# Layer 2's second block of rows: a step's seven w_ch1 products in one run, its w_ch2 products in one run

## The chip, the cores and the metric

One core of one Trainium2 chip runs the whole program once. The metric is device time in microseconds (us), from the program's start to its end. Times below come from three timed runs of the kernel before and from one profiled execution of it; in the trace, times count from the start of the span.

## The reference, cut to what matters

Three layers follow each other: a retention attention, a gated unit (`moe`), and a plain two-matrix layer (`moe2`). The change concerns the last one:

```python
def _moe2_ref(x, g_ln, w_ch1, w_ch2):          # x: (4, 576, 512)
    mu = np.mean(x, axis=-1, keepdims=True)
    var = np.mean((x - mu) ** 2, axis=-1, keepdims=True)
    xn = (x - mu) / np.sqrt(var + 1e-06) * g_ln
    ch = np.maximum(xn @ w_ch1, 0.0) @ w_ch2   # w_ch1: 512 x 2048, w_ch2: 2048 x 512
    return (x + ch)
```

## The kernel before

The 2304 rows are 18 tiles of 128, worked on as three blocks of six tiles (blocks 0, 1, 2; 768 rows each). Every fp32 product is made of three fast ones: each operand is kept as a rounded high piece (ScalarE's cast) and a low piece (the operand minus the high piece), and `mm3` multiplies high by high, high by low and low by high, one matmul each.

For `xn @ w_ch1` a scheme of seven products in place of eight is used: rows and columns are halved, sums and differences of the weight pieces (`mix_w1`) and of the features (`mix_features`) are formed first, and `HIDDEN` names the seven products. One product is 6 matmuls with 384 columns into one of two free PSUM banks. VectorE and ScalarE add the partial results (`u`, `t`), take the relu into `h` (high piece on ScalarE, low piece on VectorE).

The work of layer 2 is a row of 24 steps `s`: 8 steps for each block, a step for each pair of 128 hidden units. Steps 0 to 7 are block 0, steps 8 to 15 block 1, steps 16 to 23 block 2. Blocks 0 and 1 multiply `h` by `w_ch2` at once (`project`): six PSUM banks `o_t` hold the sums of the block, and four calls per step (`q` = 0 to 3, 9 matmuls of 512 columns each) add to them. Block 2 keeps all its hidden values (`hidden_kept`) and multiplies at the end (`multiply_kept`), with pieces of `w_ch2` that `turn_steps` and `save_w2` have written to `wb_dram` before.

Nothing is scheduled by a tool: each engine takes its instructions in the order in which the code issues them, so the loop over `s` and `q` at the end of the kernel is the schedule. In step `s` each quarter `q` issues a part of `hidden(s)` (its two, two, two and one products), then `project(s - 1, q)`, and then the work around it:

- `split_w2`: the pieces of `w_ch2` (ScalarE cast L944, GpSimd subtraction L945) for one of the two tiles `w2_at`; `load_w2` and `save_w2` load the next and store the pieces (SyncE's DMA queue).
- `fetch_w1`: from step 8 on the pieces of `w_ch1` come back from `ws_dram`, which block 0 wrote.
- `ahead(blk, q)`: the rows of the next block, by a counter `q` that runs from 0 to 31 over a block's eight steps: load (`load_y`), normalise and transpose (`norm`), store to `z_dram`, load as features (`load_features`), scale; from 24 on `mix_features` (GpSimd, L1029) and `split_features` (ScalarE cast L1036, GpSimd subtraction L1037), one of each in a quarter.
- `turning`: the differences of the pieces of `w_ch2` for block 2, by a table of quarters: two loads, four GpSimd subtractions (L961), four casts (L964), four low pieces (L967), four stores.

Rows of 128 x 512 that are loaded or stored around the blocks share seven tiles (`row_tile`), taken in turn.

Of the kernel before, what the change touches and what calls it, by code (L numbers as in the profile page):

```python
# [31 lines left out]
TB = 6  # L32
# [69 lines left out]
def kernel(  # L102
# [878 lines left out]

    def norm(p, n):
        z = yh[n]

        def stats():
            st = numbers(p)
            yield from rstd(p, st, z, 1e-6)
            after(1, lambda: newton(st))

            def rest():  # L990
                normed(z, st)
                yield
                t = row_tile()
                dve.transpose(out=t, in_=z)
                nc.sync.dma_start(out=z_dram[n], in_=t)

            after(2, rest)

        after(0, stats)
# [173 lines left out]
    def relu(s, i, v):  # L1173
        t = h_t[s, i] = h_at[i][s % len(h_at[i])]
        act.activation(out=t[:, 0], in_=v, func=ACTF.Relu)  # L1175
        dve.scalar_tensor_tensor(  # L1176
# [3 lines left out]
    def hidden(s):  # L1180
# [5 lines left out]
        for part in ((0, 5), (1, 2), (3, 4), (6,)) if s else ((5, 0, 2, 4), (1,), (3,), (6,)):  # L1186
            for w in part:
# [9 lines left out]
                elif w == 2 or w == 4:  # L1197
                    dve.tensor_tensor(out=t, in0=v, in1=u if w == 2 else t, op=ALU.add)
                    if w == 4:
                        relu(s, 3, t)  # L1200
                else:
# [4 lines left out]
                    relu(s, {1: 0, 3: 2, 6: 1}[w], v)  # L1206
                if last:
                    free(bk[a])
            yield

# [48 lines left out]
    def project(s, q):  # L1259
# [4 lines left out]
        if p == 0 and q == 0:  # L1264
            o_t[blk] = [bank() for j in range(TB)]
        first, last = p == 0 and i == 0, p == NQ - 1 and i == 1
        w = w2_at[i]
        for j in reversed(range(TB // 2)):
# [3 lines left out]
            if last:  # L1272
                n = blk * TB + h * TB // 2 + j

                o = row_tile()
                dve.tensor_tensor(
                    out=turned_row(o), in0=ps.rearrange("p (f k c) -> p f k c", k=KE, c=32),
                    in1=o_s.pop(n).rearrange("p (f k c) -> p f k c", k=KE, c=32), op=ALU.add,
                )
                free(ps)  # L1280
                store_row(n, o)
# [112 lines left out]
    def ahead(blk, q):  # L1394
# [4 lines left out]
        if q == 1 and blk:  # L1399
            for j in reversed(range(TB // 2, TB)):  # L1400
                load_rest((blk - 1) * TB + j)
        if blk + 1 < NB:
# [25 lines left out]
        if q == 4 * NQ - 1:  # L1428
            for j in reversed(range(TB // 2)) if blk + 1 < NB else range(TB):
                load_rest(blk * TB + j)  # L1430
            if blk + 1 == NB:
                o_s[None] = row_tile()
# [30 lines left out]
    for s in range(NB * NQ):  # L1463
        if s == NK:
            keep()
        steps = hidden(s) if s < NK else hidden_kept(s)
        for q in range(4):
            next(steps)
            if 0 < s <= NK:
                project(s - 1, q)  # L1470
            if s >= NQ:
                next(turns, None)

            if q == 0 and s > 1:
                split_w2(2 * s - 1)
            if q == 1 and s > 1:
                load_w2(2 * s + 1)
                save_w2(2 * s - 1)
            if q == 2 and s:
                split_w2(2 * s)  # L1480
            if q == 3 and s:
                load_w2(2 * s + 2)
# [19 lines left out]
            ahead(*divmod(4 * s + q, 4 * NQ))  # L1502
            if q < 2 and s:
# [5 lines left out]
            else:  # L1509
                fetch_w1(s + 2, q - 1)  # L1510
    for _ in multiply_kept(NB - 1):
# [61 lines left out]
```

## Time and profile before

| what | value |
|---|---|
| median of 3 runs | 657.61 us (657.12 to 658.17) |
| the profiled execution, and its span | 658.18 us, 656.2 us |
| TensorE matmul, busy in the span | 646.8 us (99%) |
| VectorE, ScalarE, GpSimd, busy | 455.0 us (69%), 316.0 us (48%), 321.6 us (49%) |
| DMA | 181.22 MB, 276 GB/s over the span |
| granted TensorE clock | full in every slice |

The profiled execution has 2.0 us outside its span. Block 0 of layer 2 begins at 282 us, step 8 at 399 us, step 16 at 525 us, and the last product of `w_ch1` ends at 591 us. In rows of the trace, PE is TensorE, DVE VectorE, ACT ScalarE, POOL GpSimd, SPq the queue of SyncE, which issues the DMAs; `b` is any PSUM bank, `w` any of the tiles for weights, `fe` the pieces of the features.

### The profile page before, as it was taken

Reading aid. Unit: us, or ns where it says so; the run is one execution under the profiler, and the core shown is the slowest. Engines: PE = TensorE matmul, PEld = TensorE weight load, DVE = VectorE, ACT = ScalarE, POOL = GpSimd, SP = SyncE. Lnnn points to the kernel's source line nnn. Section 1 sums busy time; section 2 is a strip of 40 time slices with the busy share of each in tenths; the row PEclk is TensorE's granted clock in tenths of the full one; section 3 lists DMA queues with packets and bytes.
Section 4 is the critical chain, followed back from the end, with each engine's and each line's share of the span. In section 5 each row is a group of like instructions: output and inputs, shape, how many; then the busy total and the mean of one; then the engine's idle time right before and its main releaser. Section 6 shows DMA issues by size and latency. Waiting matters only on the chain.

```text
span 656.2 us, 12551 instructions
## 1 busy us (share of the span) xinstructions
PE 646.8 (99%) x4422; PEld 591.2 (90%) x4422; DVE 455.0 (69%) x906; ACT 316.0 (48%) x656; POOL 321.6 (49%) x315
## 2 busy tenths in 40 slices
PE   8998999999999999999999999999999999999997
PEld 5998899899889889899888999888988899999996
DVE  4698779789989885868888533555533345458894
ACT  4556795365286466434453533233535313335443
POOL 2467868225326528945655793265559743310000
PEclk9999999999999999999999999999999999999999
DMA  8999447777797695489896867799999699999634
GB/s 306 383 368 371 166 111 213 252 238 233 259 298 232 189 242 145 151 312 384 319 309 238 274 205 261 247 366 387 347 332 360 216 295 350 371 379 405 243 129 161
DMA packets 99264, 181.22 MB, mean 276 GB/s; under 512 B 9857, under 2 KB 46849, under 8 KB 97410
## 3 DMA queue, kind: packets, MB, share of 16 engines
q1 hardware_dynamic: 99202, 180.42, 81.5%
q8 instruction: 35, 0.57, 0.3%
q14 instruction: 27, 0.22, 0.1%
HBM read 122.97 MB, written 56.62 MB: 274 GB/s over the span
## 4 chain that ended last, share of the span: by engine, by line
PE 71%; DVE 3%; ACT 3%; DMA 1%; issue 1%; POOL 1%; SPq 0%; POOLq 0%; ACTq 0%; DVEq 0%
PE b L137 20%; PE b L136 20%; PE b L135 20%; PE b L864 4%; PE b L1341 3%; PE b L1342 2%; DVE c L163 1%; DMA raw<-in_w_ch_dram 1%; ACT t L695 1%; PE b L798 1%; POOL vnl L721 1%; PE b L797 0%; ACT t L692 0%; ACT raw L160 0%; DVE bs L669 0%
## 5 line engine op out<-in xcount | busy, mean ns | idle before, releaser
L137 PE MATMUL b<-fe,w 128*128 128x384 f32 x336 | 113.1, 337 | 0.0
L135 PE MATMUL b<-fe,w 128*128 128x384 f32 x336 | 112.9, 336 | 0.0
L136 PE MATMUL b<-fe,w 128*128 128x384 f32 x336 | 112.7, 335 | 0.0
L137 PE MATMUL b<-w,h 128*128 128x512 f32 (+1 forms) x270 | 98.1, 363 | 0.0
L136 PE MATMUL b<-w,h 128*128 128x512 f32 (+1 forms) x270 | 98.0, 363 | 0.0
L135 PE MATMUL b<-w,h 128*128 128x512 f32 (+1 forms) x270 | 96.8, 358 | 0.0
L945 POOL TENSOR_TENSOR w<-raw_w,w 128x512 fp32r<-128x512 f32 x30 | 39.6, 1320 | 59.0 <-ACT w L944 53.3
L135 PEld LDWEIGHTS b<-fe,w 128*128 128x128 f32 x336 | 63.1, 188 | 3.0
L136 PEld LDWEIGHTS b<-fe,w 128*128 128x128 f32 x336 | 63.1, 188 | 2.8
L137 PEld LDWEIGHTS b<-fe,w 128*128 128x128 f32 x336 | 63.0, 188 | 0.0
L137 PEld LDWEIGHTS b<-w,h 128*128 128x128 f32 x270 | 51.0, 189 | 7.6
L160 ACT ACTIVATE raw<-raw 128x512 f32<-128x512 f32 x44 | 29.9, 679 | 56.2 <-DVE b L158 49.3
L136 PEld LDWEIGHTS b<-w,h 128*128 128x128 f32 x270 | 50.9, 189 | 6.3 <-POOL w L945 0.2
L135 PEld LDWEIGHTS b<-w,h 128*128 128x128 f32 x270 | 51.0, 189 | 6.0 <-issue 0.2
L1175 ACT ACTIVATE h<-b 128x384 fp32r<-128x384 f32 x32 | 15.7, 492 | 83.8 <-DVE b L1204 54.1
L665 POOL TENSOR_TENSOR st<-st,par 128x1 f32<-128x1 f32 x36 | 22.1, 617 | 52.7 <-DVE st L664 52.2
L1176 DVE SCALAR_TENSOR_TENSOR h<-b,h 128x384 fp32r<-128x384 f32 x32 | 17.8, 556 | 30.9 <-ACT h L1175 30.9
L137 PE MATMUL b<-w_sg,vnl 128*128 128x288 f32 x128 | 37.8, 295 | 0.2 <-POOL vnl L721 0.2
L135 PE MATMUL b<-w_sg,vnh 128*128 128x288 f32 x128 | 37.8, 295 | 0.0
L137 PE MATMUL b<-xt_hi,w_in 128*128 128x288 f32 x128 | 37.7, 295 | 0.0
L136 PE MATMUL b<-w_sg,vnh 128*128 128x288 f32 x128 | 37.7, 295 | 0.0
L136 PE MATMUL b<-xt_lo,w_in 128*128 128x288 f32 x128 | 37.7, 294 | 0.0
(199 smaller groups left out, 1700.8 us busy)
## 6 DMA issues: line engine op xcount, KB each, us to landing
w<-ws_dram SPq DMA_DIRECT2D x96, 256.0 KB, 4.8
raw<-in_w_ch_dram SPq DMA_DIRECT2D x32, 512.0 KB, 5.0
ws_dram<-w SPq DMA_DIRECT2D x16, 896.0 KB, 7.4
w<-wb_dram SPq DMA_DIRECT2D x14, 1024.0 KB, 5.6
qv<-in_attn_dram SPq DMA_DIRECT2D x15, 576.0 KB, 6.8
w_dram<-c SPq DMA_DIRECT2D x32, 256.0 KB, 3.1
wb_dram<-fe SPq DMA_DIRECT2D x32, 256.0 KB, 5.1
kk<-in_attn_dram SPq DMA_DIRECT2D x15, 544.0 KB, 7.7
```

Of the source, the lines that this page charges most:

```text
L135: pe.matmul(ps, lh, rh, start=first, stop=False, skip_group_check=True)
L136: pe.matmul(ps, lh, rl, start=False, stop=False, skip_group_check=True)
L137: pe.matmul(ps, ll, rh, start=False, stop=last, skip_group_check=True)
L160: act.activation(out=f(w1), in_=f(w1), func=ACTF.Square)
L163: dve.scalar_tensor_tensor(out=f(c), in0=f(w1), scalar=F64_LEAST ** 2, in1=f(r), op0=ALU.is_ge, op1=ALU.mult)
L665: pool.tensor_tensor(out=st[:, 4:5], in0=st[:, 3:4], in1=col(par, O_MH), op=ALU.pow)
L864: pe.matmul(ps, g, wo[k][:, w], start=done[0] == 1, stop=done[0] == 3 * KE, skip_group_check=True)
L945: pool.tensor_tensor(out=t[:, 1], in0=raw, in1=f(t[:, 0]), op=ALU.subtract)
L1175: act.activation(out=t[:, 0], in_=v, func=ACTF.Relu)
L1176: dve.scalar_tensor_tensor(out=t[:, 1], in0=v, scalar=0.0, in1=f(t[:, 0]), op0=ALU.max, op1=ALU.subtract)
L1341: pe.matmul(ps, e[:, 0, x], t, start=begin, stop=False, skip_group_check=True)
L1342: pe.matmul(ps[:, 0:256], e[:, 1, x], t[:, 0:256], start=False, stop=end, skip_group_check=True)
```

## The change

For steps 8 to 15 a new function `hidden_once` issues all seven products of a step in one run (order 0, 5, 1, 2, 4, 3, 6) with a pause after the first two, in which the pieces of `w_ch2` for this same step are made: `split_w2` of both tiles. Then `project` of this step (not of the step before) follows in one run of 36 matmuls, in the order `q` = 3, 2, 0, 1; within one call the three kinds of product are now outermost and the tile `j` innermost. The four calls of `ahead`, with the turning, stand between the four calls of `project`, so all four come behind the seven products of their step. Step 7 ends with the projection of step 7 itself, in one run of 36. Step 16 has none any more.

Around it: the first result of a step passes through a tile `z` in SBUF, so that its bank comes free before its relu; `save_w2` stores from step 4 to step 11 instead of 8 to 15; the table of `turning` starts one piece every 6 quarters instead of 4 for the first five, with 4 quarters between load and use; the stores of normalised rows are collected and issued at the end of a step or ahead of the load that needs them; `load_rest` and the features' loads and scaling are called at other quarters.

```diff
     def save_w2(s):
-        if NF <= s < 2 * NK:
-            p, i = divmod(s - NF, 2)
+        if NQ <= s < NF + NQ:
+            p, i = divmod(s % NF, 2)
...
+    def hidden_once(s):
...
+        for w in (0, 5, 1, 2, 4, 3, 6):
+            x, a, first, last = HIDDEN[w]
+            if first:
+                bk[a] = bank()
+            product(s, bk[a], w, x, first, last)
+            v = bk[a][:, 0:TH]
+            if w == 0:
+                act.copy(u, v)
+            elif w == 1:
+                dve.tensor_scalar(out=z, in0=v, scalar1=0.0, scalar2=None, op0=ALU.max)
...
+            if last and w != 3:
+                free(bk[a])
+            if w == 5:
+                yield
+        relu_low(s, 2, bk[2][:, 0:TH])
+        free(bk[2])
+        relu_low(s, 0, z)
+        relu_low(s, 1, u)
+        yield
...
-    def project(s, q):
+    def project(s, q, begin=0):
...
+        for x, y in ((0, 0), (0, 1), (1, 0)) if begin and not last else ():
+            for j in js:
+                pe.matmul(
...
-            if q in (13, 20):
-                load_features(blk + 1, q // 20)
-            if q in (15 + blk, 22 + blk):
+            if q in (13, 20 - blk):
+                store_z()
+                load_features(blk + 1, q // 19)
+            if q in (15 + 2 * blk, 22 + blk):
...
-            start, pace = (3 + 4 * p, 1) if p < 5 else (8 * p - 8, 2)
-            for o in (0, 1, 1, 2, 2, 3, 4, 5):
+            start, pace = (3 + 6 * p, 1) if p < 5 else (34 + 8 * (p - 5) - p // 7, 2)
+            for o in (0, 4, 4, 5, 5, 8, 8, 9) if p < 5 else (0, 1, 1, 2, 2, 3, 4, 5):
...
-        steps = hidden(s) if s < NK else hidden_kept(s)
+        if s < NQ:
+            steps = hidden(s)
+        elif s < NK:
+            steps = hidden_once(s)
+            next(steps)
+            split_w2(2 * s + 1)
+            split_w2(2 * s)
+            load_w2(2 * s + 3)
+            load_w2(2 * s + 2)
+            next(steps)
+        else:
+            steps = hidden_kept(s)
         for q in range(4):
-            next(steps)
-            if 0 < s <= NK:
+            if NQ <= s < NK:
+                project(s, (3, 2, 0, 1)[q], 1)
+            else:
+                next(steps)
+            if 0 < s < NQ:
                 project(s - 1, q)
...
             ahead(*divmod(4 * s + q, 4 * NQ))
+            if NQ <= s < NK:
+                next(turns, None)
...
+        store_z()
+        if s == NQ - 1:
+            split_w2(2 * s + 1)
+            load_w2(2 * s + 3)
+            save_w2(2 * s + 1)
+            for q in range(4):
+                project(s, q)
```

Three places show how the instructions stand now. The first is TensorE inside a step of block 1. Rows with `fe` are products of `w_ch1`, rows with `h` products of `w_ch2`; the brackets name whom an instruction waits for. Before, the end of one call of `project` and the product behind it:

```order
L135 MATMUL b_76<-w_3373,h 128x512
L136 MATMUL b_76<-w_3373,h 128x512
L137 MATMUL b_76<-w_3373,h 128x512
L135 MATMUL b_79<-fe,w_3466 128x384 [waits DMAHW2_49,DVE_49]
L136 MATMUL b_79<-fe,w_3466 128x384
```

And now, the end of a step's second product (5) and the beginning of its third (1):

```order
L135 MATMUL b_79<-fe,w_3466 128x384
L136 MATMUL b_79<-fe,w_3466 128x384
L137 MATMUL b_79<-fe,w_3467 128x384
L135 MATMUL b_81<-fe,w_3466 128x384 [waits DMAHW6_49,Activation_49]
L136 MATMUL b_81<-fe,w_3466 128x384
```

A product follows a product now, with no projection between them, and the third waits for ScalarE's copy of the first one's result out of the same bank.

The second place is GpSimd in steps 14 and 15, where the features of block 2 are mixed and split (`mix`, `fe`), the pieces of `w_ch2` made (`w_3373`), and now some of the turning done (`raw_turn`). Before:

```order
L945 TENSOR_TENSOR w_3373<-raw_w_5348,w_3373 128x512
L1029 TENSOR_TENSOR mix<-x 128x768
L1037 TENSOR_TENSOR fe<-x,fe 128x768
L1029 TENSOR_TENSOR mix<-x,mix 128x768
L1037 TENSOR_TENSOR fe<-mix,fe 128x768
L945 TENSOR_TENSOR w_3373<-raw_w_5411,w_3373 128x512
L1029 TENSOR_TENSOR mix<-x,mix 128x768
L1037 TENSOR_TENSOR fe<-mix,fe 128x768
L1029 TENSOR_TENSOR mix<-x 128x768
L1037 TENSOR_TENSOR fe<-mix,fe 128x768
L945 TENSOR_TENSOR w_3373<-raw_w_5480,w_3373 128x512
```

And now:

```order
L945 TENSOR_TENSOR w_3373<-raw_w_5339,w_3373 128x512
L1038 TENSOR_TENSOR mix<-x 128x768
L1046 TENSOR_TENSOR fe<-x,fe 128x768
L1038 TENSOR_TENSOR mix<-x,mix 128x768
L1046 TENSOR_TENSOR fe<-mix,fe 128x768
L961 TENSOR_TENSOR raw_turn<-raw_turn 128x256 x2
L1038 TENSOR_TENSOR mix<-x,mix 128x768
L1046 TENSOR_TENSOR fe<-mix,fe 128x768
L961 TENSOR_TENSOR raw_turn<-raw_turn 128x256 x2
L1038 TENSOR_TENSOR mix<-x 128x768
L1046 TENSOR_TENSOR fe<-mix,fe 128x768
L945 TENSOR_TENSOR w_3373<-raw_w_5466,w_3373 128x512
```

Two pairs of turning subtractions stand among the mixing and splitting of step 14, and both pieces of `w_ch2` for step 15 (the last row is the first of them) stand behind all of it.

The third place is ScalarE between step 14 and step 15: relus of `h`, casts of `fe`, and the copy of the first product's result into `u`. Before:

```order
L944 CAST w_3373<-raw_w_5411 128x512 [waits DMAHW2_49,DMAHW3_49,PE_49,Activation_49]
L1036 CAST fe<-mix 128x768 [waits Pool_49]
L1175 ACTIVATE h<-u 128x384 [waits DVE_49,Activation_49]
L1036 CAST fe<-mix 128x768 [waits Pool_49]
L1194 COPY u<-b_78 128x384 [waits PE_49]
```

And now:

```order
L1184 ACTIVATE h<-b_79 128x384 [waits DVE_49]
L1184 ACTIVATE h<-u 128x384 [waits DVE_49,Activation_49]
L1045 CAST fe<-x 128x768
L1045 CAST fe<-mix 128x768 [waits Pool_49] x3
L1239 COPY u<-b_81 128x384 [waits PE_49]
```

All four casts of step 14 now stand behind its last relu, and the copy of step 15 behind the last of the three that wait for GpSimd's mixing.

## Rows read from the trace of the kernel before

**Rows 1.** The page, part 1: each engine's busy time, share of the span, instructions.

```profile
PE 646.8 (99%) x4422; PEld 591.2 (90%) x4422; DVE 455.0 (69%) x906; ACT 316.0 (48%) x656; POOL 321.6 (49%) x315
```

**Rows 2.** Waits of TensorE's weight loads: total us, times, longest.

```profile
PEld b L519 <- ACT zero L515: 2.3, 1, 2.3
...
PEld b L136 <- POOL w L945: 0.2, 1, 0.2
```

**Rows 3.** Timeline of TensorE in step 9: start, us, engine, line, tiles.

```profile
425.69 0.50 PE L136 MATMUL b<-w,h 128*128 128x512 f32 x1
426.03 0.40 PE L137 MATMUL b<-w,h 128*128 128x512 f32 x1
...
426.96 0.39 PE L135 MATMUL b<-w,h 128*128 128x512 f32 x1
...
427.64 0.33 PE L135 MATMUL b<-fe,w 128*128 128x384 f32 x1
```

**Rows 4.** Timeline of TensorE, last quarters of step 15: where the runs begin.

```profile
519.80 0.39 PE L135 MATMUL b<-w,h 128*128 128x512 f32 x1
...
521.88 0.33 PE L135 MATMUL b<-fe,w 128*128 128x384 f32 x1
...
522.94 0.39 PE L135 MATMUL b<-w,h 128*128 128x512 f32 x1
...
525.02 0.33 PE L135 MATMUL b<-fe,w 128*128 128x384 f32 x1
```

**Rows 5.** Timeline of TensorE in block 2: two of its products' matmuls, 78 apart.

```profile
541.80 0.33 PE L135 MATMUL b<-fe,w 128*128 128x384 f32 x1
...
555.32 0.33 PE L135 MATMUL b<-fe,w 128*128 128x384 f32 x1
```

**Rows 6.** The chain that ended last: a run of 512-column matmuls of the layer before.

```profile
268.57 13.62 PE b L864 x60
```

**Rows 7.** Timeline of GpSimd in block 1: start, us, line, tiles.

```profile
468.93 1.56 POOL L961 TENSOR_TENSOR raw_turn<-raw_turn 128x256 f32<-128x256 f32 x2 [3.35 <-DMA raw_turn<-w_dram]
470.44 1.29 POOL L945 TENSOR_TENSOR w<-raw_w,w 128x512 fp32r<-128x512 f32 x1
...
498.24 1.85 POOL L1029 TENSOR_TENSOR mix<-x 128x768 f32<-128x768 f32 x1
500.04 1.85 POOL L1037 TENSOR_TENSOR fe<-x,fe 128x768 fp32r<-128x768 f32 x1
501.84 1.84 POOL L1029 TENSOR_TENSOR mix<-x,mix 128x768 f32<-128x768 f32 x1
...
509.61 2.16 POOL L1037 TENSOR_TENSOR fe<-mix,fe 128x768 fp32r<-128x768 f32 x1
```

**Rows 8.** Timeline of ScalarE around step 15.

```profile
509.68 0.84 ACT L1036 CAST fe<-mix 128x768 fp32r<-128x768 f32 x1 [1.06 <-POOL mix L1029]
510.58 0.48 ACT L1194 COPY u<-b 128x384 f32<-128x384 f32 x1
...
523.79 0.53 ACT L1175 ACTIVATE h<-u 128x384 fp32r<-128x384 f32 x1 [0.89 <-DVE u L1204]
524.22 0.82 ACT L1036 CAST fe<-x 128x768 fp32r<-128x768 f32 x1
```

**Rows 9.** Timeline of VectorE around step 15.

```profile
508.65 1.42 DVE L1176 SCALAR_TENSOR_TENSOR h<-u,h 128x384 fp32r<-128x384 f32 x1 [0.65 <-ACT h L1175]
...
523.14 0.56 DVE L1204 TENSOR_TENSOR u<-b,u 128x384 f32<-128x384 f32 x1 [0.89 <-PE b L137]
```

**Rows 10.** Block 2: its stretch (engines' busy us, clock, DMA share, GB/s).

```profile
541.00:591.00 50.00, 50.00 (x290) 50.00 (x289) 27.23 (x51) 17.58 (x41) 14.38 (x20) 1.00 1.03 365
```

**Rows 11.** Timeline of SyncE's queue: the last of `fetch_w1`'s issues for steps 22 and 23.

```profile
573.92 2.31 SPq L931 DMA_DIRECT2D w<-ws_dram  x4
```

**Rows 12.** DMA issues of 541 to 591 us: count, KB each, median us to landing.

```profile
w<-ws_dram SPq DMA_DIRECT2D x32, 256.0 KB, 4.9
```

**Rows 13.** Timeline of TensorE: the first matmul of step 23's products.

```profile
584.44 0.33 PE L135 MATMUL b<-fe,w 128*128 128x384 f32 x1
```

More of the change, by code (lines that the diff above doesn't have):

```diff
@@ L980, in load_y, with store_z @@
         nc.sync.dma_start(out=yh[n], in_=y_dram[n])
+    z_out = []
+    def store_z():
+        for n, t in z_out:
+            nc.sync.dma_start(out=z_dram[n], in_=t)
+        z_out.clear()
     def norm(p, n):
@@ L994, in rest @@
                 dve.transpose(out=t, in_=z)
-                nc.sync.dma_start(out=z_dram[n], in_=t)
+                z_out.append((n, t))
+                if p is t1 or n < 2 * TB:
+                    store_z()
             after(2, rest)
@@ L1175, in relu, with relu_low @@
         act.activation(out=t[:, 0], in_=v, func=ACTF.Relu)
+    def relu_low(s, i, v):
+        t = h_t[s, i]
         dve.scalar_tensor_tensor(
@@ L1200, in hidden @@
                         relu(s, 3, t)
+                        relu_low(s, 3, t)
                 else:
@@ L1209, in hidden @@
             yield
+    def hidden_once(s):
+        u = t2.tile([128, TH], F32, tag="u", name="u")
+        t = t2.tile([128, TH], F32, tag="v", bufs=1, name="t")
+        z = t2.tile([128, TH], F32, tag="z", bufs=1, name="z")
+        bk = {}
+        for w in (0, 5, 1, 2, 4, 3, 6):
[8 more added lines that the diff above has]
+                dve.tensor_scalar(out=z, in0=v, scalar1=0.0, scalar2=None, op0=ALU.max)
+            elif w == 2 or w == 4:
+                dve.tensor_tensor(out=t, in0=v, in1=u if w == 2 else t, op=ALU.add)
+                if w == 2:
+                    relu(s, 0, z)
+                else:
+                    relu(s, 3, t)
+            elif w == 3:
+                dve.tensor_tensor(out=v, in0=v, in1=u, op=ALU.add)
+                relu(s, 2, v)
+                relu_low(s, 3, t)
+            else:
+                dve.tensor_tensor(out=u, in0=v, in1=u, op=ALU.add)
+                if w == 6:
+                    relu(s, 1, u)
+            if last and w != 3:
[7 more added lines that the diff above has]
+        yield
     def hidden_kept(s):
@@ L1263, in project @@
         t = h_t.pop((s, q))
-        if p == 0 and q == 0:
+        if blk not in o_t:
             o_t[blk] = [bank() for j in range(TB)]
-        first, last = p == 0 and i == 0, p == NQ - 1 and i == 1
+        first, last = p == 0 and i == begin, p == NQ - 1 and i != begin
         w = w2_at[i]
-        for j in reversed(range(TB // 2)):
+        js = list(reversed(range(TB // 2)))
+        for x, y in ((0, 0), (0, 1), (1, 0)) if begin and not last else ():
+            for j in js:
+                pe.matmul(
+                    o_t[blk][h * TB // 2 + j], t[:, x, j * 128:(j + 1) * 128], w[:, y], start=first and x == y,
+                    stop=False, skip_group_check=True,
+                )
+        for j in () if begin and not last else js:
             c = slice(j * 128, (j + 1) * 128)
@@ L1271, in project @@
             mm3(ps, t[:, 0, c], t[:, 1, c], w[:, 0], w[:, 1], first, last)
[L1272 to L1281, printed above, removed]
+            if not last:
+                continue
+            n = blk * TB + h * TB // 2 + j
+            o = row_tile()
+            dve.tensor_tensor(
+                out=turned_row(o), in0=ps.rearrange("p (f k c) -> p f k c", k=KE, c=32),
+                in1=o_s.pop(n).rearrange("p (f k c) -> p f k c", k=KE, c=32), op=ALU.add,
+            )
+            free(ps)
+            store_row(n, o)
     def load_rest(n):
@@ L1398, in ahead @@
         n = (blk + 1) * TB
-        if q == 1 and blk:
-            for j in reversed(range(TB // 2, TB)):
-                load_rest((blk - 1) * TB + j)
+        if q in (28, 29) and blk + 1 < NB:
+            for j in reversed(range(TB // 2)):
+                load_rest(blk * TB + (q - 28) * TB // 2 + j)
         if blk + 1 < NB:
@@ L1427, in ahead @@
                 next(feat[1])
-        if q == 4 * NQ - 1:
-            for j in reversed(range(TB // 2)) if blk + 1 < NB else range(TB):
+        if q == 4 * NQ - 1 and blk + 1 == NB:
+            for j in range(TB):
                 load_rest(blk * TB + j)
-            if blk + 1 == NB:
-                o_s[None] = row_tile()
+            o_s[None] = row_tile()
     def keep():
```

28 lines of the change are left out of this document (18 added, 10 removed).

## The prediction

> **What bounds the kernel now.** The page's first part comes first: TensorE is busy for 646.8 of 656.2 us [rows 1]. Next I read who waits for whom, TensorE and its weight loads alone: of twelve rows of the second kind, the longest from the program's start, one is a wait for another engine in layer 2, 0.2 us, for GpSimd's pieces of `w_ch2` [rows 2]. So in block 1 TensorE runs without a gap, and only two things can move the time: how closely its matmuls follow each other, and new waits of TensorE. The rest (fewer stores here, a collected store there) costs or gives nothing unless it becomes such a wait.
>
> The timeline shows how closely they follow. A call of `project`, 9 matmuls, lasts from 519.80 to 521.88, 2.08 us, 231 ns each; the six matmuls after it last 1.06 us, 177 ns each; then 2.08 us again [rows 4]. In long runs both are faster: 78 matmuls of 384 columns in 13.52 us, 173.3 ns each [rows 5], and 60 of 512 columns in 13.62 us, 227 ns each [rows 6]. So each change between the two kinds costs something: 2.08 - 9 x 0.227 = 0.04 us for `project`, 1.06 - 6 x 0.1733 = 0.02 us for the products behind it (0.025 unrounded), 0.065 us a pair. The one wait of step 9 shows that `project` itself can run at 227 ns: after it the matmuls from 426.96 to 427.64 take 0.68 us for three [rows 3].
>
> **What the change gives.** Before, `project` stands in 64 runs (steps 1 to 16, four each). Now there are 27 of 9 matmuls in steps 1 to 7, one of 45 at step 7's end, and eight of 36: 28 pairs of changes fewer. If a run of 36 settles to 227 ns soon after its ninth matmul, that is 28 x 0.065 = 1.8 us. If it stayed at 231 ns for good, only the products' part would come back, 28 x 0.025 = 0.7 us. After its wait step 9 settled within six matmuls, so I take 1.6. The wait of step 9 itself (425.69 to 426.03, 0.34 instead of 0.23 us) goes, 0.11 us: its GpSimd piece stood behind a turning step that waited for its load, and now four quarters lie between the two. Gain: 1.7 us.
>
> **What it costs.** I went through the order of ScalarE, VectorE and GpSimd step by step, asking which instruction TensorE needs soonest. For steps 8 to 13 each wait has cover: within the run of products a bank is free again about 0.8 us after its product ends (VectorE begins 0.20 us after, 523.14 against 522.94, and takes 0.56 [rows 4, 9]), and the next product covers 1.04 us. These six steps cost nothing; if a VectorE instruction of 0.6 us stood ahead of that addition, each would lose some 0.4 us. Pieces of `w_ch2` have five products, 5.2 us, for a cast and two GpSimd subtractions of 1.29 us [rows 7].
>
> Steps 14 and 15 are different. In step 14 GpSimd mixes and splits block 2's features. ScalarE's four casts for them used to lie a quarter apart, between products; now all stand behind the step's last relu, and step 15's copy of its first result stands behind them. TensorE's third product of step 15 adds into the bank that this copy reads. Count from P, where step 14's 36 `project` matmuls begin:
>
> - VectorE's last addition begins at P + 0.20 [rows 4, 9], the relu 0.65 later, the first cast 0.43 after that and lasts 0.82 [rows 8]: GpSimd can take its first low piece at P + 2.15.
> - GpSimd then works in its order: low piece, mix, low piece, two turning subtractions, third mix. The steps of 1.80 and 1.51 us are those from start to start [rows 7]: 3 x 1.80 + 1.51 + 1.85 = 8.76, so the third mix ends at P + 10.91.
> - ScalarE casts it and begins the copy 0.90 later (509.68 to 510.58), which takes 0.48 [rows 8]: P + 12.29, and TensorE goes on at about P + 12.35.
> - TensorE would want that bank at P + 8.21 (36 matmuls) + 1.07 + 1.04 = P + 10.32.
>
> That is a wait of 2.03 us. In the kernel before the same copy began the moment the cast was over, at 510.58, 0.2 us after its product ended: there was no spare time for the 1.51 us of turning that now stands ahead of the mix. Where VectorE and GpSimd work at once, a low piece took 2.16 instead of 1.85 us while a VectorE instruction took 1.42 instead of 0.56 [rows 7, 9]; VectorE's last low pieces of `h` fall on GpSimd's first one here, so I add 0.31: **2.35 us**, between 1.7 (a turning pair partly hidden) and 3.2.
>
> The Trainium skill goes further (SBUF — State Buffer, Terms, the shared port pair): VectorE and GpSimd take these ports for a whole instruction in turn, and the loser stands still. That speaks against `z`, which sends one more relu per step through SBUF. By that rule each such VectorE instruction would set GpSimd back by its whole length; the trace shows 0.31 of 0.56 us. With three of them in steps 14 and 15 each at full length the time would be that of the third rival below.
>
> Then a second wait. After the third mix GpSimd has a low piece, two turning subtractions, the fourth mix, a low piece and only then the first piece of `w_ch2` for step 15: 3 x 1.80 + 1.51 + 1.29 = 8.20 us. TensorE, going on 1.44 us after the mix's end, has five products (5.2) and three matmuls (0.69) before it needs that piece: 7.33. **0.9 us**, between 0.5 and 1.4 by the same overlap. The second piece is asked for only after 18 more matmuls, and the features that follow have 1.9 us to spare at step 16's third product.
>
> Sum: 2.35 + 0.9 - 1.7 = +1.5 us. The profiled execution, 656.2 of span and 658.18 in all, would have 659.7; it stood 0.57 above the median, so the median goes from 657.61 to **659.1 us**. With gains of 0.8 to 1.9 and costs of 2.2 to 4.6 the forecast's own range is 657.9 to 661.4. A difference of 0.2%, 1.3 us, is about what the measurement of this kernel can tell from none.
>
> **Rivals.**
>
> 1. Faster: the copy comes in time. Place: ScalarE between steps 14 and 15. It needs the third mix to end by about P + 8.9 (10.32 less 1.44), 2.0 us sooner than I work out; from there down TensorE never waits. Then the pieces of `w_ch2` would also be in time, and 1.7 us remain as gain: 655.9. For it: before, the casts just came in time. Against it: GpSimd's row of five instructions with no wait in it. 0.13.
> 2. DMA becomes the bound in block 2. There the DMA engines are full already, 1.03 of their time at 365 GB/s [rows 10]. One more turned piece is stored there now, 1 MB, 2.9 us at that rate, and step 16 loses the 8.3 us of `project`. The last fetches that step 23 begins with were issued at 573.92 to 576.2, landed 4.9 us later, by 581.1, and were needed from 584.44 [rows 11 to 13]: 3.3 us to spare. The two together exceed it, unless some of the backlog is made up on the way: a further 2 us, 661.1. Against it: blocks 0 and 1 take over stores. 0.14.
> 3. VectorE and GpSimd hold each other up by whole instructions, where I count 0.31 us once: three times 0.56 us in the two chains instead, 1.7 - 0.31 = 1.4 more: 660.5. For it the 1.42 us row; against it the 2.16. 0.10.
> 4. The change comes to nothing: the waits are as short as their lower bounds (2.2) and the gain is full (1.9): +0.3, 657.9, which the forecast's own lower end holds.
>
> **How the numbers follow.** The forecast, both waits with a sum of +0.3 to +3.8, gets 0.63. Its middle lies just above the 1.3 us mark, so 0.36 of it is slower and 0.27 within. Rival 1 is 0.11 faster and 0.02 within. Rivals 2 and 3 are slower, 0.24. That makes faster 0.11, within 0.29, slower 0.60; since I cannot exclude a gain that no row shows, I move 0.02 from slower to faster. For 8 in 10 I leave out rival 1's time at the lower end and, above the forecast's own range, rivals 2 and 3 coming together: 656.3 to 661.4.
>
> **What would show it.** In the profile after, TensorE's waits would have two new rows: for ScalarE's copy (about 2.3 us, once, in step 15) and for GpSimd's pieces of `w_ch2` (about 0.9 us, once). In steps 8 to 14, 36 matmuls of `project` would last 8.2 us (right) or 8.3 (they do not settle), 42 of the products 7.3. GpSimd would be busy without a gap from step 14's relu to the middle of step 16. I am wrong if the third mix of step 14 ends less than 9 us after that step's `project` begins, if TensorE waits for VectorE in steps 8 to 13, or if a fetch of `w_ch1` lands late in block 2.

## The result and the profile after

The changed kernel takes 667.37 us (median of 6 runs, 665.24 to 669.92), the kernel before 657.89 us in the same session (6 runs, 657.09 to 659.66): 1.0141 times as long, 95% interval 1.0114 to 1.0168. The forecast was 659.1, at most 661.4. The sign was right and the size wrong: 9.5 us were lost where 1.5 were expected.

Three rows of the changed kernel's page answer to [rows 1]: the first part, and of the forty slices TensorE's granted clock (in tenths of full speed) and the DMA engines' share.

```profile
PE 649.3 (98%) x4422; PEld 592.9 (89%) x4422; DVE 455.2 (68%) x914; ACT 317.9 (48%) x656; POOL 320.8 (48%) x315
...
PEclk9999999999999999999999999999999899989999
DMA  8999447677878695399988888888999589999634
```

TensorE's busy time grew by 2.5 us, so 6.4 of the 8.9 us by which the span grew are time in which it stands still. Its clock fell in two slices. The waits of TensorE's matmuls and, in the second fence, of its weight loads (total us, times, longest) answer to [rows 2]:

```profile
PE b L135 <- ACT u L1280: 3.5, 1, 3.5
...
PE b L135 <- ACT u L1239: 1.8, 1, 1.8
PE b L135 <- DMA w<-ws_dram: 1.3, 1, 1.3
```

```profile
PEld b L135 <- ACT u L1280: 3.9, 1, 3.9
...
PEld b L135 <- ACT u L1239: 2.1, 1, 2.1
PEld b L135 <- DVE b L1291: 1.6, 1, 1.6
```

L1239 is ScalarE's copy of a step's first product in `hidden_once`, the wait that was forecast for step 15. L1280 is the same copy in `hidden_kept`, in block 2, where none was forecast. The last row of each fence is one and the same wait in step 18, told below. Two stretches, step 15 with its `project` and block 2 (columns as in [rows 10]):

```profile
516.00:535.00 19.00, 17.24 (x79) 15.48 (x79) 8.34 (x15) 7.76 (x15) 18.17 (x15) 0.91 0.54 185
542.00:600.00 58.00, 53.07 (x294) 51.77 (x293) 27.45 (x51) 20.05 (x46) 20.29 (x28) 0.97 1.02 363
```

**Where the 8.9 us between the two profiled spans (656.2 and 665.1) come from.** I compared where the same matmul begins in both traces. From the first product of layer 2 to the last it takes 318.87 instead of 309.51 us, 9.36 more; the layer began 0.5 us earlier by chance, and what follows it takes 64.68 us in both. Of the 9.36:

- step 15's products, 515.82 to 526.74, take 10.92 instead of 7.31 us: +3.61;
- block 2, from step 17's first product to step 23's last, takes 58.14 (542.25 to 600.39) instead of 50.81: +7.33;
- short waits in step 5 add 0.18;
- the rest, -1.76, is the gain.

**The gain** is what was worked out. Timeline of TensorE in step 8 (the row stands for 36 matmuls):

```profile
414.40 8.36 PE L1326 MATMUL b<-w,h 128*128 128x512 f32 x36
```

The next products begin at 422.60, 8.20 us after this run; within it the starts are 224 to 236 ns apart for nine matmuls (231 on average, as in [rows 4]), and 226 or 227 from there to the end. Steps 8 to 13 show no wait.

**Step 15.** GpSimd around it, answering to [rows 7], and then ScalarE, answering to [rows 8]. P, where step 14's `project` begins, is 507.62.

```profile
509.79 1.84 POOL L1046 TENSOR_TENSOR fe<-x,fe 128x768 fp32r<-128x768 f32 x1 [2.61 <-ACT fe L1045]
511.59 1.84 POOL L1038 TENSOR_TENSOR mix<-x,mix 128x768 f32<-128x768 f32 x1
513.39 1.85 POOL L1046 TENSOR_TENSOR fe<-mix,fe 128x768 fp32r<-128x768 f32 x1
515.20 1.56 POOL L961 TENSOR_TENSOR raw_turn<-raw_turn 128x256 f32<-128x256 f32 x2
516.72 1.83 POOL L1038 TENSOR_TENSOR mix<-x,mix 128x768 f32<-128x768 f32 x1
...
525.36 2.87 POOL L945 TENSOR_TENSOR w<-raw_w,w 128x512 fp32r<-128x512 f32 x2
```

```profile
518.58 0.83 ACT L1045 CAST fe<-mix 128x768 fp32r<-128x768 f32 x1 [4.27 <-POOL mix L1038]
519.32 0.47 ACT L1239 COPY u<-b 128x384 f32<-128x384 f32 x1
```

The third mix ends at 518.55, P + 10.93, where 10.91 was worked out. TensorE's next matmul begins at 519.84, 1.92 us late. But then its matmuls of 384 columns, which are 173 ns apart, go to 320 ns, ten of them (the second number is a modelled length; the starts count):

```profile
521.41 0.52 PE L137 MATMUL b<-fe,w 128*128 128x384 f32 x1
521.73 0.52 PE L135 MATMUL b<-fe,w 128*128 128x384 f32 x1
...
524.29 0.51 PE L137 MATMUL b<-fe,w 128*128 128x384 f32 x1
```

384 columns in 320 ns is 1.2 GHz, the lower of the two levels. The granted clock, 0.91 over the whole stretch above, is 0.50 in these 3.2 us (the last three numbers are clock, DMA share and GB/s):

```profile
521.40:524.60 3.20, 3.20 (x11) 3.20 (x11) 0.91 (x2) 0.53 (x1) 3.20 (x3) 0.50 0.97 340
```

That is 10 x 0.147 = 1.5 us, which no part of the forecast held. It also hid the second wait: GpSimd had its first piece of `w_ch2` ready at about 526.8, and `project`, now late, began at 526.74.

**Block 2.** ScalarE's casts for the turned `w_ch2` (L964) wait for the transfers that empty the staging tiles, and in step 22 they stand ahead of the copy that TensorE needs. ScalarE there, then TensorE on both sides of the longest gap:

```profile
583.87 0.41 ACT L964 CAST fe<-raw_turn 128x256 fp32r<-128x256 f32 x1 [2.73 <-DMA wb_dram<-fe]
585.06 1.18 ACT L964 CAST fe<-raw_turn 128x256 fp32r<-128x256 f32 x3 [0.78 <-DMA wb_dram<-fe]
586.15 0.47 ACT L1280 COPY u<-b 128x384 f32<-128x384 f32 x1
```

```profile
582.79 0.34 PE L137 MATMUL b<-fe,w 128*128 128x384 f32 x1
586.67 0.69 PE L135 MATMUL b<-fe,w 128*128 128x384 f32 x1 [3.54 <-ACT u L1280]
587.16 0.52 PE L136 MATMUL b<-fe,w 128*128 128x384 f32 x1
587.48 0.52 PE L137 MATMUL b<-fe,w 128*128 128x384 f32 x1
```

Step 22 loses 3.70 us in the gap and 1.4 in the slow matmuls behind it, 5.1 in all. The other 2.2 are a gap of 1.50 us at 555.86 and short ones in steps 17 to 19, all for late fetches of `w_ch1`:

```profile
557.54 0.41 PE L135 MATMUL b<-fe,w 128*128 128x384 f32 x1 [1.34 <-DMA w<-ws_dram]
```

The fetch that this matmul waits for was issued at 551.15, right behind the fifth piece's stores (548.40 to 551.06), and landed at 557.40. The weight load's row of 1.6 us above names VectorE for the same wait, but that addition was over at 556.80. In step 18 ScalarE's casts wait for stores too, but no matmul waits for ScalarE there.

The transfers that the casts of step 22 wait for were issued by SyncE only just before. Its queue in the changed kernel around steps 15, 18 and 21, then the kernel before: the seventh piece's stores on SyncE and the eighth piece's casts on ScalarE:

```profile
520.49 1.05 SPq L931 DMA_DIRECT2D w<-ws_dram  x2
532.46 0.52 SPq L1311 DMA_DIRECT2D out_dram<-row  x1
...
548.40 2.66 SPq L970 DMA_DIRECT2D wb_dram<-fe  x4
551.15 8.48 SPq L931 DMA_DIRECT2D w<-ws_dram  x12
...
574.49 4.26 SPq L931 DMA_DIRECT2D w<-ws_dram  x6
578.85 2.47 SPq L970 DMA_DIRECT2D wb_dram<-fe  x4
581.37 0.91 SPq L1358 DMA_DIRECT2D w<-wb_dram  x1
```

```profile
567.06 2.38 SPq L970 DMA_DIRECT2D wb_dram<-fe  x4
569.53 2.05 SPq L931 DMA_DIRECT2D w<-ws_dram  x4
```

```profile
577.30 1.32 ACT L964 CAST fe<-raw_turn 128x256 fp32r<-128x256 f32 x4
578.52 0.48 ACT L1225 COPY u<-b 128x384 f32<-128x384 f32 x1
```

Before, the stores were issued 10 us ahead of the casts, and these found the staging tiles empty. Now they are issued at 578.85 to 581.3, and the casts want the tiles at 581.14, when the relu before them ends. On ScalarE the casts have kept their place, behind the last relu of step 21, 7.6 us into that step (before: 7.4). It is the stores that moved: they began 2.8 us ahead of step 21's first product and now begin 5.3 us behind it, 8.1 us later. Two quarters of this, 3.6 us, stand in the table, which stores the seventh piece at quarter 52 of blocks 1 and 2 (before: 50) and casts the eighth at 55 (before: 54). The rest is SyncE's queue, which now runs some 4.4 us late against TensorE.

### The profile page after: what moved, and what is told of

It is laid out like the page before. It is cut to its first block, busy times and chain, and to the rows that moved or that the text cites. A ratio compares the mean times of both kernels' runs of the same rounds, so it can differ in the third digit from the quotient of the medians.

```text
span 665.1 us, 12568 instructions
## 1 busy us (share of the span) xinstructions
PE 649.3 (98%) x4422; PEld 592.9 (89%) x4422; DVE 455.2 (68%) x914; ACT 317.9 (48%) x656; POOL 320.8 (48%) x315
## 4 chain that ended last, share of the span: by engine, by line
PE 49%; DMA 8%; POOL 2%; issue 2%; SPq 2%; DVE 1%; ACT 1%; POOLq 0%; DVEq 0%; ACTq 0%
PE b L137 12%; PE b L135 12%; PE b L136 12%; PE b L1326 7%; DMA w<-ws_dram 3%; PE b L1404 3%; PE b L864 2%; PE b L1405 2%; DMA w_dram<-c 1%; DMA x_r<-x_dram 1%; DMA wb_dram<-fe 1%; SPq L842 1%; DMA raw_turn<-w_dram 1%; POOL w L945 1%; DMA raw_w<-w_dram 1%
## 5 line engine op out<-in xcount | busy, mean ns | idle before, releaser
L135 PE MATMUL b<-fe,w 128*128 128x384 f32 x336 | 114.4, 340 | 6.6 <-ACT u L1280 3.5
L137 PE MATMUL b<-fe,w 128*128 128x384 f32 x336 | 114.2, 340 | 0.0
L136 PE MATMUL b<-fe,w 128*128 128x384 f32 x336 | 113.9, 339 | 0.0
L135 PEld LDWEIGHTS b<-fe,w 128*128 128x128 f32 x336 | 64.1, 191 | 9.7 <-ACT u L1280 3.9
L136 PEld LDWEIGHTS b<-fe,w 128*128 128x128 f32 x336 | 63.9, 190 | 1.4
L137 PEld LDWEIGHTS b<-fe,w 128*128 128x128 f32 x336 | 64.0, 190 | 0.7 <-DMA w<-ws_dram 0.7
L1326 PE MATMUL b<-w,h 128*128 128x512 f32 x270 | 62.8, 390 | 0.0
L137 PE MATMUL b<-w,h 128*128 128x512 f32 (+1 forms) x180 | 62.3, 346 | 0.0
L136 PE MATMUL b<-w,h 128*128 128x512 f32 (+1 forms) x180 | 62.2, 346 | 0.0
L135 PE MATMUL b<-w,h 128*128 128x512 f32 (+1 forms) x180 | 61.8, 343 | 0.0
L1326 PEld LDWEIGHTS b<-w,h 128*128 128x128 f32 x270 | 50.6, 188 | 10.2
L137 PE MATMUL b<-xt_hi,w_in 128*128 128x288 f32 x128 | 37.7, 295 | 0.0
L137 PEld LDWEIGHTS b<-w,h 128*128 128x128 f32 x180 | 34.1, 189 | 4.1
L135 PE MATMUL b<-xt_hi,w_in 128*128 128x288 f32 x128 | 37.7, 294 | 0.0
L1253 DVE TENSOR_TENSOR u<-b,u 128x384 f32<-128x384 f32 x16 | 8.9, 557 | 42.0 <-PE b L137 31.8
```

The lines of the kernel that those rows point to most:

```text
L135: pe.matmul(ps, lh, rh, start=first, stop=False, skip_group_check=True)
L136: pe.matmul(ps, lh, rl, start=False, stop=False, skip_group_check=True)
L137: pe.matmul(ps, ll, rh, start=False, stop=last, skip_group_check=True)
L1253: dve.tensor_tensor(out=u, in0=v, in1=u, op=ALU.add)
L1326: pe.matmul(o_t[blk][h * TB // 2 + j], t[:, x, j * 128:(j + 1) * 128], w[:, y], start=first and x == y, stop=False, skip_group_check=True,)
```

## The experiments

After this reading there were three theories on block 2's 7.3 us. **A**: SyncE is held by the row stores of block 1's last `project` (nothing issued from 521.5 to 532.46, the DMA engines at 0.54), and the backlog is carried on. **B**: the turning table alone. **C**: the wait of step 15 shifts the engines against each other. Interval below: the 95% interval of the ratio to the kernel before, whose median in these sessions was 657.4 to 658.0 us.

**e1_rows_late.**

```diff
             free(ps)
-            store_row(n, o)
+            if s < NK - 1:
+                store_row(n, o)
+            else:
+                held.append((n, o))
...
+            if s == NK and q == 1:
+                for x in held:
+                    store_row(*x)
```

> The changed kernel (667.4 us), with one thing changed: the stores of the six rows of the last project of block 1 are collected and issued in step 16, behind the fetches of its second quarter, so that the SyncE queue is no longer held by them at the end of step 15. Theory A (the held queue: 10.6 us in which SyncE waits for the evictions while the DMA engines are half idle, and the backlog is carried through block 2): stage from 542 to 600 falls from 58.2 to 51 to 53 us, the time to 660 to 662; what stays is the wait and the slow clock of step 15, about 3.5 us. Theory B (the turning table alone: one more piece of w_ch2 and a shorter gap for the turning stage in block 2): 666 to 668, the waits of ScalarE's casts for the turned stores stay at about 10 us. Theory C (the wait in step 15 shifts the engines against each other and makes the later waits): 666 to 668 too.

665.59 us, 1.0120 (1.0105 to 1.0135). Block 2 takes 57.0 us instead of 58.1, and the copy of step 22 still comes 3.63 us late. SyncE's queue shows why:

```profile
520.23 1.06 SPq L931 DMA_DIRECT2D w<-ws_dram  x2
531.26 2.41 SPq L970 DMA_DIRECT2D wb_dram<-fe  x4
```

With the row stores gone, the next instruction in line, the fourth piece's stores, is issued at 531.26, 1.2 us sooner than the row stores were: it waits for GpSimd, which is late itself. The row named at the head of a queue was not what held it. The queue still stood for 10 us, so this run alone doesn't settle theory A; e2 does.

**e2_old_table**: the turning table of before in the changed kernel.

```diff
-            start, pace = (3 + 6 * p, 1) if p < 5 else (34 + 8 * (p - 5) - p // 7, 2)
-            for o in (0, 4, 4, 5, 5, 8, 8, 9) if p < 5 else (0, 1, 1, 2, 2, 3, 4, 5):
+            start, pace = (3 + 4 * p, 1) if p < 5 else (8 * p - 8, 2)
+            for o in (0, 1, 1, 2, 2, 3, 4, 5):
```

> The changed kernel with the turning table of the kernel before (pieces start 4 quarters apart, offsets 0 to 5; five pieces are stored before block 2 begins, and no subtraction stands among the feature mixes). Theory A (held SyncE queue): the wait of step 15 shrinks (third mix ends about 1.7 us sooner or more), about 3 us back, and of block 2's 7.2 us only the one piece (2.9 us of transfers): 661 to 664. Theory B (the table alone): block 2 back at 51 us and step 15's wait nearly gone: 656 to 658. Theory C (the wait of step 15 makes the later ones): 656 to 658.

664.40 us, 1.0099 (1.0082 to 1.0117). Block 2 is clean (TensorE busy without a gap, at full clock):

```profile
548.00:598.00 50.00, 50.00 (x291) 50.00 (x290) 27.19 (x51) 17.62 (x42) 17.32 (x24) 1.00 1.03 359
```

But TensorE waits three times earlier, 1.56 us in step 13, 4.12 in step 14 and 0.54 in step 15, with nine matmuls at 320 ns behind the second. All of a step's quarters now lie within the 8.2 us of `project`, so the old offsets, with 2 quarters from a piece's stores to the next piece's casts, leave a cast too little time:

```profile
503.36 0.41 ACT L964 CAST fe<-raw_turn 128x256 fp32r<-128x256 f32 x1 [7.09 <-DMA wb_dram<-fe]
505.70 1.18 ACT L964 CAST fe<-raw_turn 128x256 fp32r<-128x256 f32 x3 [1.93 <-DMA wb_dram<-fe]
```

So block 2's loss is the table's, as B says. A falls: SyncE stands here from 527.5 to 538.08, with the row stores at its head, as long as in the changed kernel. C falls too: TensorE waited in steps 13 and 14 and block 2 lost nothing. The price of the old table in the new order was foreseen by none of the three.

**e3_rows_table**: both edits together.

> Both: the changed kernel with the row stores of the last project of block 1 issued in step 16, and the turning table of the kernel before. Theory A: the queue is free and one piece less lies in block 2: 655.5 to 657, below the kernel before by the 1.7 us of the fewer changes between runs. Theory B: the same as with the old table alone, 656 to 658, the two within 0.7 us of each other. Theory C: the same as the old table alone.

666.24 us, 1.0126 (1.0111 to 1.0142): no better than the table alone, with the same kind of waits (2.48 and 3.09 us in steps 13 and 14, both followed by slow matmuls) and a clean block 2.

**e4_subs_early.**

```diff
-            for o in (0, 4, 4, 5, 5, 8, 8, 9) if p < 5 else (0, 1, 1, 2, 2, 3, 4, 5):
+            for o in (0, 1, 1, 2, 2, 8, 8, 9) if p == 3 else (0, 4, 4, 5, 5, 8, 8, 9) if p < 5 else (0, 1, 1, 2, 2, 3, 4, 5):
```

> The changed kernel with its own table, but the fourth piece's four subtractions on GpSimd at quarters 22 and 23 instead of 25 and 26, away from the feature mixes; its casts, low parts and stores stay where they are. The wait of step 15 was 1.9 us, with 0.2 us to start again and 1.6 us of matmuls at half clock behind it. Theories A and B: those 3.5 us come back and block 2 still takes 57 to 58 us: 663.5 to 665. If the clock falls there for a reason other than the wait: 665.5. Theory C (the wait shifts the engines and so makes block 2's waits): 656 to 659.

668.53 us, 1.0169 (1.0144 to 1.0193), a miss. The wait of step 15 is gone, but one quarter between a piece's load and its subtraction is too little; GpSimd stands, `w_ch2`'s pieces come late, and `project` waits 3.71 us in step 14:

```profile
504.84 1.56 POOL L961 TENSOR_TENSOR raw_turn<-raw_turn 128x256 f32<-128x256 f32 x2 [13.21 <-DMA raw_turn<-w_dram]
```

The slow clock came along: `project`'s other 33 matmuls take 10.49 us from start to start (512.76 to 523.25), where 33 x 0.227 = 7.5.

**e5_before_table**: one part of the change alone, the new table in the kernel before (the table's two lines, the other way round).

> The kernel before with one part of the change alone: the changed kernel's turning table. The order of the products, the saving of w_ch2 in steps 8 to 15 and all else are as before. If the table makes block 2's loss by itself: the stage from the start of step 17 to the last product of layer 2 grows from 51 us by 4 to 7 us, and the time is 661 to 665. If it needs the changed order around it (row stores of project at the end of step 15 and all of a step's instructions in one go): 657.5 to 659.

663.76 us, 1.0087 (1.0057 to 1.0117). Nearly the whole loss, 6.1 us, stands in step 22, which takes 13.4 instead of 7.3 us: the copy 3.31 us late, then 16 matmuls at 320 ns. The table needs nothing else of the change to lose this. SyncE is late here too: the seventh piece's stores begin at 574.59, 4.4 us behind step 21's first product. In step 15 the subtractions among the mixes cost this kernel 0.2 us, where the changed order cost 3.6.

**e6_last_piece**: the eighth piece one quarter later.

```diff
-            start, pace = (3 + 6 * p, 1) if p < 5 else (34 + 8 * (p - 5) - p // 7, 2)
+            start, pace = (3 + 6 * p, 1) if p < 5 else (34 + 8 * (p - 5), 2)
```

> The changed kernel with the last turned piece one quarter later (start 50 instead of 49), so that its casts are 4 quarters behind the stores of the piece ahead, as in the kernel before, instead of 3, and stand behind the step's copy on ScalarE instead of ahead of it. If these 3 quarters (5.5 us, with the stores issued 2.4 to 5 us late and landing 3 to 6 us after) make the wait of step 22: its 3.7 us and the 1.6 us of half clock behind it go, and the time falls to 661.5 to 663; step 15 and the waits of steps 18 and 19 stay. If DMA throughput is the limit there, another wait of the same size takes its place, and the time is 666 to 668.

663.19 us, 1.0078 (1.0056 to 1.0100). The copy comes in time. That is ScalarE's order as much as the distance: the casts, now behind the copy (582.41), still wait 1.64 us for the stores. And a smaller wait takes its place, for the fetches of `w_ch1`, which stand behind the late stores on SyncE's queue: 2.57 us at step 22's end, with no slow matmuls behind it.

```profile
PE b L135 <- DMA w<-ws_dram: 3.2, 2, 2.4
PE b L135 <- ACT u L1239: 2.4, 1, 2.4
```

**e7_subs_late.**

```diff
-            for o in (0, 4, 4, 5, 5, 8, 8, 9) if p < 5 else (0, 1, 1, 2, 2, 3, 4, 5):
+            for o in (0, 6, 6, 7, 7, 8, 8, 9) if p == 3 else (0, 4, 4, 5, 5, 8, 8, 9) if p < 5 else (0, 1, 1, 2, 2, 3, 4, 5):
```

> The changed kernel with the fourth piece's subtractions on GpSimd at quarters 27 and 28, behind the last feature mix, instead of 25 and 26 between the mixes (its loads, casts and stores stay). The third mix then ends about 3 us sooner after project begins, ahead of ScalarE's copy. If GpSimd's order makes the wait of step 15: no wait there, and no matmuls at half clock behind it, 663 to 664. If the half-speed matmuls have another cause: 665.5. If a wait for w_ch2's pieces on GpSimd takes its place (the forecast's second wait, 0.5 to 1.4 us), 664 to 665.

666.35 us, 1.0127 (1.0097 to 1.0156); in its profile block 2 loses 9.0. Step 15 behaves as worked out: the third mix ends at P + 9.58 (506.26 to 515.84), the copy's wait falls to 0.56 us, no matmul there is slow, and the forecast's second wait appears, 1.37 us from start to start:

```profile
PE b L135 <- ACT u L1280: 4.0, 1, 4.0
PE b L135 <- DMA w<-ws_dram: 1.5, 1, 1.5
PE b L1326 <- POOL w L945: 1.2, 1, 1.2
PE b L135 <- ACT u L1239: 0.4, 1, 0.4
```

**e8_all_three**: e1, e6 and e7 together.

> The changed kernel with the last piece one quarter later, the fourth piece's subtractions behind the last mix, and the row stores of the last project of block 1 issued in step 16. If the three places are the whole loss: block 2 at 51 to 52 us, no wait in step 15: 655.5 to 657.5, at or below the kernel before. If the DMA engines' work sets block 2's time: 659 to 663.

663.95 us, 1.0089 (1.0054 to 1.0125). Block 2 takes 56.4 us with the DMA engines at 1.04: there the copies come in time, the fetches of `w_ch1` don't (2.49 us in step 22, and slow matmuls). In step 15 the copy is 1.10 us late and GpSimd's piece 1.37 us. The three places weren't the whole loss.

**e9_new_table**: a third table.

```diff
-            start, pace = (3 + 6 * p, 1) if p < 5 else (34 + 8 * (p - 5) - p // 7, 2)
-            for o in (0, 4, 4, 5, 5, 8, 8, 9) if p < 5 else (0, 1, 1, 2, 2, 3, 4, 5):
+            start, pace = ((0, 4, 9, 14, 22)[p], 1) if p < 5 else (8 * p - 8, 2)
+            for o in (
+                (0, 4, 4, 5, 5, 8, 8, 9) if p < 4 else (0, 6, 6, 7, 7, 9, 9, 10) if p == 4 else (0, 1, 1, 2, 2, 3, 4, 5)
+            ):
```

> The changed kernel with a third turning table, all five first pieces stored before step 17: starts 0, 4, 9, 14, 22 with the changed kernel's offsets (the fifth: subtractions at quarters 28 and 29, behind the feature mixes and the step's w_ch2 pieces; casts 31, stores 32), the last three as in the kernel before. Stores and the next piece's casts are at least 4 quarters apart everywhere. Theory now (the table's extra piece and late starts fill the DMA engines in block 2; the subtractions among the mixes make step 15's wait): block 2 at 51 us, step 15 with at most 0.6 us of waits and no half clock, so the gain of the fewer changes is left: 655.5 to 657, 0.1 to 0.4% under the kernel before. If the changed order of the products itself costs something in block 2 or step 15: 658 to 661.

657.30 us (12 runs), 0.9995 (0.9980 to 1.0010): all of the loss is back, and no more than that can be told from the kernel before. In its profile (span 655.1) block 2 takes 51.5 us and TensorE's matmuls have one wait for another engine in blocks 1 and 2, the copy of step 15 (0.54 us from start to start):

```profile
539.00:590.00 51.00, 50.83 (x292) 50.20 (x292) 27.34 (x51) 17.91 (x42) 17.31 (x24) 1.00 1.05 372
```

```profile
PE b L135 <- ACT u L1239: 0.4, 1, 0.4
```

From the first product to the last it takes 309.24 us, with 0.65 us in step 15, 0.70 in block 2 and 0.31 in block 0 that are waits: 307.6 without them, 1.8 below the kernel before without its wait of step 9 (309.4). The gain exists; these waits use up nearly all of it. One pair of pieces in this table is only 3 quarters apart (stores at quarter 9, casts at 12, in steps 10 and 11), against what was expected, and nothing waits there: quarters alone do not tell whether stores are done.

**e10_stores_moved**: the amount in block 2 against the distance between stores and casts.

```diff
-        for j, t in enumerate(stage):
-            nc.sync.dma_start(out=wb_dram[j, p // 4, :, p % 4], in_=f(t))
+        for n in {3: (3, 4), 4: ()}.get(p, (p,)):
+            for j, t in enumerate(stage):
+                nc.sync.dma_start(out=wb_dram[j, n // 4, :, n % 4], in_=f(t))
```

> The changed kernel with the fifth piece's stores taken out of block 2: its place in the turned matrix is filled in step 15 from the fourth piece, so the output isn't the reference's; everything else, the 3 quarters between the seventh piece's stores and the eighth's casts too, stays. 1 MB less to move in block 2, 2.9 us of the DMA engines at the rate measured. If the amount of transfers in block 2 sets step 22's wait: it shrinks by about 2.9 us to under 1 us and the half clock behind it goes, 662 to 663.5. If the distance of 3 quarters sets it: the 3.7 us stay, only the waits of steps 18 and 19 go (2 to 2.5 us), 664.5 to 665.5.

664.96 us, 1.0106 (1.0086 to 1.0126), by its time what the distance would give, but not by its waits. Step 22's gap halves, 3.70 to 1.90 us, and stays, with ten slow matmuls: the step loses 3.6 us instead of 5.1. The late fetches of steps 18 and 19 didn't go either, but came sooner: step 17 loses 2.0 us and step 18 0.4. SyncE issued the fourth piece's stores together with the ones moved only at 534.86 to 540.17, so the amount was moved ahead of block 2 by a few us and no more.

**e11_old_tail**: the changed kernel's table for the first five pieces, that of before for the last three.

```diff
-            start, pace = (3 + 6 * p, 1) if p < 5 else (34 + 8 * (p - 5) - p // 7, 2)
+            start, pace = (3 + 6 * p, 1) if p < 5 else (8 * p - 8, 2)
```

> The changed kernel with its own table for the first five pieces (the fifth is stored in step 17) and the table of the kernel before for the last three (casts and stores 2 quarters sooner than now). The amount moved in block 2 is that of the changed kernel, the distances are those of the kernel before except 2 quarters between the fifth piece's stores and the sixth's casts. If the distance sets step 22's wait: it goes, and a shorter one than 1.5 us comes in step 17 or 18, 661 to 663. If the amount sets it: a wait of 2 to 4 us in block 2 stays, 664 to 667.

669.83 us, 1.0169 (1.0141 to 1.0196). Step 22 has no wait; the gap went to step 18, where the sixth piece's casts now follow the fifth's stores by 2 quarters: 4.36 us, then 13 slow matmuls. The fifth's stores were issued at 552.84, 7.9 us behind step 17's first product and just as the casts wanted the tiles. With e10: the gap comes where casts stand closest behind stores, and in e10, with less to move, it is shorter. Neither run changes one of the two alone.

**e12_best**: e9 with two edits more.

```diff
-            if q >= 24 and q != 28:
+            if q >= 24 and q != 28 - blk:
```

and the late row stores of e1.

> The third table (657.3 us) with two edits more: the feature work leaves out quarter 27 instead of 28, so that only two mixes stand ahead of ScalarE's copy of step 15, and the row stores of the last project of block 1 are issued in step 16, behind the fetches of its second quarter. The first should take away the last wait of step 15 (0.54 us), the second the late fetches at the start of step 18 (two waits of 0.35 us each). If both do: 655.8 to 656.6, 0.15 to 0.3% under the kernel before. If the row stores only move the DMA engines' work within a full stage, the late fetches stay: 656.3 to 657.2.

661.52 us (10 runs, 658.37 to 666.87), 1.0050 (1.0028 to 1.0071), a miss. The copy of step 15 does come in time. In the profiled run, its slowest, two other waits came: 2.36 us in step 18, for fetches that now stand behind the row stores, and 3.25 us in step 14, where ScalarE's scaling stands ahead of the copy and waits for its loads:

```profile
503.63 2.13 ACT L1024 ACTIVATE x<-x,par 128x384 f32<-128x384 f32 x4 [8.42 <-DMA x<-z_dram]
505.67 0.45 ACT L1239 COPY u<-b 128x384 f32<-128x384 f32 x1
```

In e9 the same scaling ends at 500.20 and the copy begins at 501.28, 1.1 us later: the changed order leaves that little there. None of e12's edits stands ahead of this place, so they didn't cause it in an obvious way; whether e9 shows it in some of its runs was not profiled.

## Why the prediction was wrong

- **The gain** (1.7 us) was right: 1.76 in the changed kernel, 1.8 in e9, and a run of 36 settled after nine matmuls.
- **Steps 8 to 13 cost nothing**: right for the kernel as changed. The cover was the table's as much as the order's: with the old offsets e2 and e3 wait 1.56 and 2.48 us in step 13.
- **The first wait** (2.35 us) was right in place, chain and size: 1.92 in the changed kernel, 2.52 to 2.57 in e1, e6, e10 and e11, where this stretch is unedited. (The four terms given for the first low piece add up to P + 2.10, not 2.15; it began at P + 2.17.) With the 1.5 us of subtractions out of the chain the third mix came 1.4 us sooner (e7). What the step lacked was the price behind the wait: about 1.5 us of matmuls at half clock.
- **The second wait** (0.9 us) did not show, since that slow stretch gave GpSimd the time. Where the stretch runs at full speed it is there, 1.37 us (e7), the upper end of 0.5 to 1.4.
- **The step that failed is the sum's silence on block 2.** The prediction took the DMA engines as full there [rows 10], and the second rival asked that fullness one question only, whether the fetches of `w_ch1` land in time, with 3.3 us to spare [rows 11 to 13]: a further 2 us at 0.14. It never followed the table's last three pieces. The sixth and seventh piece's stores now stand two quarters later and SyncE issues them later still, so ScalarE's casts, which kept their place, met stores that had only just been issued, and ScalarE works in order, with TensorE's copy behind them. 7.3 us instead of none, 5.1 of them in step 22; e5 shows 6.1 of such a loss with the table alone. The second rival's own sign, a late fetch, came true as the smaller part, 2.2 us in steps 17 to 19, and as the main one in step 22 once the casts were moved (e6, e8).
- **Third rival** (VectorE and GpSimd hold each other up by whole instructions): not in the changed kernel, where VectorE's low pieces fell into a pause of GpSimd (507.18 to 509.79) and the chain kept to its 10.91 us within 0.02; so the 0.31 us added for an overlap did not show. In e1, e6, e10 and e11 the chain took 0.6 to 0.7 more: VectorE's low piece of `h` ahead of its last addition took 1.29 to 1.32 us instead of 0.55, beside GpSimd's first mix (in e1 505.37 to 507.22). That is about half of the rival's 1.4 us, at one place instead of three. In e1:

```profile
506.31 1.32 DVE L1188 SCALAR_TENSOR_TENSOR h<-t,h 128x384 fp32r<-128x384 f32 x1
```

- **First rival**: the condition it needed, a third mix by P + 8.9, was not met, not even without the subtractions (P + 9.58, and 0.56 us of wait).

What stays open: how block 2's loss in the changed kernel divides between the times in the table and the amount to be moved, and why SyncE's queue runs late there. The runs show that both count, not by how much each.

## What to carry to other kernels

When a table of times is changed, follow every row that moves, not only those near the change's purpose: for each staging buffer compare when it is emptied with when it is next wanted, in issue times from the trace and not in the table's own units, and ask what stands behind the waiting instruction on its engine. A queue that stands still tells where to look but not what holds it: the instruction next in line may wait for the same late engine (e1). And a wait of TensorE has to be priced with the slow matmuls that may follow it.

## What the hardware showed that I had not expected

Behind most of the long waits TensorE ran on at half clock. In the profiles of the changed kernel and the twelve experiments the steps of layer 2 hold 20 waits of 1.90 to 4.36 us. Behind 18 of them, within 2 us, the half-speed matmuls come: 7 to 16 at 320 ns instead of 173, in e4 13 of 512 columns at 427 instead of 227. That is 1.0 to 2.6 us lost again. Two, of 2.57 us (e6) and 3.66 us (e4), have none behind them, and neither have the waits of 1.69, 1.56 and 1.50 us (e7, e2, the changed kernel). The Trainium skill (TensorE: Matmul & The Clock Gate, What's actually happening) says that the gate passes either half or all of the clock's pulses. The traces agree: in the changed kernel the granted clock is 0.50 from 521.4 to 524.6 us, at 320 ns for 384 columns, and 0.99 from 524.6 to 526.7, at 173.
